# Linear attention feeding a two-matrix layer on one core: attention's products regrouped by array form, projection rounds of 4, 2 and 3 tiles

## The chip, the cores and the metric

The kernel runs on one core of a Trainium2 chip. The metric is the device time of one execution in microseconds; lower is better. Before the change the median of three runs is 1205.09 us (1204.46 to 1205.18).

## The reference

What is computed, cut to what matters (8 batches, 8 heads, 576 positions, head width 64, 128 features; the layer has 512 inputs and 2048 hidden units):

```python
def phi(x):
    proj = np.einsum('bhsd,df->bhsf', x, w_phi)
    proj = proj - np.max(np.abs(proj), axis=-1, keepdims=True)
    return np.concatenate([np.exp(proj), np.exp(-proj)], axis=-1)
q_p, k_p = (phi(q), phi(k))
kv = np.einsum('bhsf,bhsd->bhfd', k_p, v)
z = np.sum(k_p, axis=2)
num = np.einsum('bhsf,bhfd->bhsd', q_p, kv)
den = np.einsum('bhsf,bhf->bhs', q_p, z)[..., None] + 1e-06
attn = num / den
# heads side by side give x, 4608 tokens x 512
h = x @ w_in
out = (h - np.tanh(h)) @ w_out
```

## The kernel before, in words

There are two stages. In the first, attention is worked through in 32 units; a unit is one pair of heads of one batch. In the second stage the two-matrix layer runs over twelve groups of three token tiles and sixteen slices of the hidden width; the change touches it in one place only (where the last unit's reciprocal is taken). The second stage's weights come as 64-bit numbers and are turned into 32-bit ones on the way through the first stage (`dec_load`, `dec_0`, `dec_1`, `dec_2`).

The first stage runs in periods, written out by hand in `period(i)` under `tc.manual_schedule()`: each engine, and SP's queue of transfers, gets its instructions in the order of the text. A period works on four units at once: `a` = unit i (projected), `c` = unit i - 1 (its features are transposed, its products with v are summed), `p` = unit i - 2 (its numerator and denominator are formed), `p2_` = unit i - 3 (its division is finished).

The steps of a unit, by function and line of the profile:

- `load` and `load_v` (L184, L188) bring q and k (tile `qk`) and `v` of the next unit on SP's queue. Both tiles have two buffers.
- `project(u, r)` (L197) multiplies three tiles of q or k with `w_phi` on PE, a product for each of the two heads on its half of the rows (form 64x128), into the one buffer `pp` of PSUM. VectorE then takes the greatest absolute value (L202) and subtracts it (L204). There are three rounds, r = 0, 1, 2; four and a half of the nine tiles are q's.
- `qt` (L210) and `qt_rest` (L216) transpose q's part on PE; `q_exp` and `q_exp_rest` (L221, L226) take the exponentials on ScalarE into `qe`. `k_exp` (L231) does it for k, into `kp`.
- `kv` (L239) and `ksum` (L247) form the products of k's features with v (forms 128x64, and 64x64 for the half tile) and their sums (128x32 and 64x32), both in `pc`. `kv_copy` (L253) and `kv_turn` (L258, L260) copy and transpose them.
- `out_heads` forms the numerators (L268, form 128x64) and the denominators (L279, form 128x32) in three buffers `po`; `out_copy` (L289, L292) copies them out.
- `den` (L297) loads the denominators from `dd`, spread over all 128 partitions, as `dn`. `den_recip` adds the small constant and takes the reciprocal on VectorE (L305, L306), stores it in memory as `rr` (L307) and loads it back, one row for each head, as `rb` (L310). `den_mul` multiplies on POOL (L315) and stores the result in `xs` (L316), from which the second stage loads its x (L105).

All these transfers go out on SP's queue. A transfer waits there for what it needs, a full buffer to send or a free buffer to fill. The order on it in one period before the change: `qk` and `v` of unit i + 1, `dn` of `p`, `xs` of `p2_`, a weight (`raw`), then `rr` and twice `rb` of `p`.

Single-precision products are two instructions each on PE, and transposes one: that is why a round of six products shows as 12.

Of the kernel before, what the change touches and what calls it, by code (L numbers as in the profile page):

```python
# [19 lines left out]
P = 128  # L20
# [12 lines left out]
def tile_linear_attention_moe(  # L33
# [83 lines left out]
    with ExitStack() as c1:  # L117
# [40 lines left out]
        def dec_0(u):  # L158
            rr = u.r.bitcast(U32).rearrange("p (n t) -> p n t", t=2)
            u.lo, u.hi = rr[:, :, 0], rr[:, :, 1]  # L160
            u.a = raw.tile([P, DM], U32, tag="dec_a", name=f"dec_a{u.nm}", bufs=2)
            nc.scalar.activation(f32(u.a), f32(u.hi), AF.Abs, scale=65536.0)

        def dec_1(u):
# [14 lines left out]

        def load(u):  # L180
            u.qk = p2.tile([P, PC], F32, tag="qk", name=f"qk{u.i}")
            w = PC if u.i else 3 * P
            for o in range(0, PC, w):
                nc.sync.dma_start(u.qk[:, o : o + w], qkT[u.i][:, o : o + w])  # L184

        def load_v(u):
            u.v = p2.tile([P, 5, 2, D], F32, tag="v", name=f"v{u.i}")
            nc.sync.dma_start(u.v.rearrange("p j e d -> p (j e d)"), v5[u.i])  # L188


        def project(u, r):
            pp = ps_pj.tile([P, 2, 512], F32, tag="pj", name=f"pp{u.i}_{r}")
            for a in range(3):
                j = 3 * r + a
                for e in range(2):
                    hs = slice(e * D, (e + 1) * D)
                    nc.tensor.matmul(  # L197
                        pp[:, e, a * F : (a + 1) * F], u.qk[hs, j * P : (j + 1) * P], wph[hs, :], start=True, stop=True
                    )
            x = pp[:, :, 0 : 3 * F].rearrange("p e (a f) -> p e a f", f=F)  # L200
            m = p2.tile([P, 2, 3], F32, tag="m", name=f"m{u.i}_{r}")
            nc.vector.tensor_reduce(m, x, AX.X, ALU.max, apply_absolute_value=True)  # L202
            t = p2.tile([P, 2, 3, F], F32, tag=f"t{r}", name=f"t{u.i}_{r}")
            nc.vector.tensor_tensor(t, x, m.unsqueeze(3).broadcast_to([P, 2, 3, F]), ALU.subtract)  # L204
            u.t[r] = t

        def qt(u, e):
            pt = ps_tr.tile([P, 512], F32, tag="tr", name=f"ptt{u.i}_{e}")
            for j in range(4):
                nc.tensor.transpose(pt[:, j * P : (j + 1) * P], u.t[j // 3][:, e, j % 3, :], ident)  # L210
            return pt

        def qt_rest(u):
            pt = ps_tr.tile([P, 512], F32, tag="tr", name=f"ptr{u.i}")
            for e in range(2):
                nc.tensor.transpose(pt[:, e * SR : (e + 1) * SR], u.t[1][0:SR, e, 1, :], ident[0:SR, 0:SR])  # L216
            return pt

        def q_exp(u, e, pt):
# [6 lines left out]
                nc.scalar.activation(u.qe[:, :, s, SM:S], x, AF.Exp, scale=1.0 - 2.0 * s)  # L226

        def k_exp(u, r):
            x, j0, j1 = (u.t[1][:, :, 1:3, :], 0, 2) if r == 1 else (u.t[2], 2, 5)
            for s in range(2):  # L230
                nc.scalar.activation(u.kp[:, :, j0:j1, s, :], x, AF.Exp, scale=1.0 - 2.0 * s)  # L231


        def kv(u):
            u.pc = ps_c.tile([P, 512], F32, tag="pc", name=f"pc{u.i}")
            for j in range(5):
                r = slice(SR, P) if j == 0 else slice(0, P)
                for e in range(2):
                    nc.tensor.matmul(  # L239
                        u.pc[e * D : (e + 1) * D, 0 : 2 * F], u.v[r, j, e, :], u.kp[r, e, j, :, :], start=(j == 0), stop=(j == 4)  # L240
                    )

        def ksum(u):
            for j in range(5):
                r = slice(SR, P) if j == 0 else slice(0, P)
                for n in range(4):
                    nc.tensor.matmul(  # L247
                        u.pc[n * 32 : (n + 1) * 32, 2 * F : 3 * F], ones[r, :], u.kp[r, n // 2, j, n % 2, :], start=(j == 0), stop=(j == 4)
                    )

        def kv_copy(u):
            u.kvt = p2.tile([P, 3, F], F32, tag="kvt", name=f"kvt{u.i}")
            u.kv_last = nc.scalar.copy(u.kvt.rearrange("p a f -> p (a f)"), u.pc[:, 0 : 3 * F])  # L253

        def kv_turn(u):
            pt = ps_d.tile([P, 512], F32, tag="po", name=f"ptk{u.i}")
            for a in range(3):
                nc.tensor.transpose(pt[:, a * P : (a + 1) * P], u.kvt[:, a, :], ident)  # L258
            u.kv = p2.tile([P, 3, P], F32, tag="kv", name=f"kv{u.i}")
            nc.vector.tensor_copy(u.kv.rearrange("p a c -> p (a c)"), pt[:, 0 : 3 * P])  # L260


        def out_heads(u):
            u.po = [ps_d.tile([P, 512], F32, tag="po", name=f"po{u.i}_{c}") for c in range(3)]
            for s in range(2):
                for c in range(2):
                    for e in range(2):
                        nc.tensor.matmul(  # L268
                            u.po[c][e * D : (e + 1) * D, 0:CH],
                            u.kv[:, s, e * D : (e + 1) * D],  # L270
                            u.qe[:, e, s, c * CH : (c + 1) * CH],
                            start=(s == 0),
                            stop=(s == 1),
                        )
            for s in range(2):
                for e in range(2):
                    for c in range(2):
                        n, w = 2 * e + c, 2 * e + s
                        nc.tensor.matmul(  # L279
                            u.po[2][n * 32 : (n + 1) * 32, 0:CH],  # L280
                            u.kv[:, 2, w * 32 : (w + 1) * 32],
                            u.qe[:, e, s, c * CH : (c + 1) * CH],
                            start=(s == 0),
                            stop=(s == 1),
                        )

        def out_copy(u):
            u.dd = tail.tile([P, CH], F32, tag="dd", name=f"dd{u.i}", bufs=2)
            nc.scalar.copy(u.dd, u.po[2][:, 0:CH])  # L289
            u.d = tail.tile([P, S], F32, tag="d", name=f"d{u.i}", bufs=2)  # L290
            for c in range(2):
                nc.scalar.copy(u.d[:, c * CH : (c + 1) * CH], u.po[c][:, 0:CH])  # L292

        def den(u):
            w = 2 * S // P
            dn = tail.tile([P, w], F32, tag="dn", name=f"dn{u.i}")
            nc.sync.dma_start(dn, u.dd.rearrange("(n r) c -> n r c", r=32)[:, 0, :])  # L297
            u.dn = dn
# [33 lines left out]
        def unit(i):  # L332
            return units[i] if 0 <= i < NU else None


        def period(i):
            a, c, p, p2_ = unit(i), unit(i - 1), unit(i - 2), unit(i - 3)
# [3 lines left out]
            if i == NU - 2:  # L341
                xt[0] = x_tiles(0)
                for j in range(NCT):
                    x_load(0, xt[0], j)
            if a:
                a.kp = p2.tile([P, 2, 5, 2, F], F32, tag="kp", name=f"kp{i}")
                if i == 0:
                    warm(16)
                project(a, 0)
            if c:  # L350
                k_exp(c, 2)
            if p:
                out_heads(p)
            if 2 <= i < NU:
                dec_0(dec[i])
                dec_1(dec[i])
            if p:
                out_copy(p)
                den(p)
            if p2_:  # L360
                den_mul(p2_)
            if 1 <= i <= 2 * AHEAD:
                split_w(i - 1)
            if i < 2:
                warm(8)
            if c and i == 1:
                kv(c)
            if a:
                project(a, 1)
            if c and i > 1:  # L370
                kv(c)
            if a:
                k_exp(a, 1)
            if 2 <= i < NU:
                dec_2(dec[i])
            if 2 <= i < NU - 2:
                dec.append(dec_load(i + 2))
            if i == 0:
                warm(8)
            if a:  # L380
# [1 line left out]
            if i < 2:  # L382
                dec_0(dec[i])
                dec_1(dec[i])
                dec_2(dec[i])
                dec.append(dec_load(i + 2))
            if c:
                c.qe = p1.tile([P, 2, 2, S], F32, tag="qe", name=f"qe{i - 1}")
                pt = qt(c, 0)
                q_exp(c, 0, pt)  # L390
                ksum(c)
                ptr = qt_rest(c)
                kv_copy(c)
                q_exp_rest(c, ptr)
                pt = qt(c, 1)
                kv_turn(c)
                q_exp(c, 1, pt)
            if p:
                den_recip(p)
            if i == NU - 1:  # L400
                for j in range(NCT):
                    x_split(xt[0], j)
# [2 lines left out]
        with tc.manual_schedule():  # L405
            for i in range(NU + 1):
                period(i)
        period(NU + 1)

    with ExitStack() as c2:
# [68 lines left out]
        for i in range(len(steps) + 2):  # L481
# [12 lines left out]
            if 1 <= i <= len(steps):  # L494
                g, f = steps[i - 1]
                gg[i - 1] = split_g(g, f, gs.pop(i - 1), G)
            if i == 2:
                den_mul(units[-1], pin)
            while late and late[0] <= 2 * AHEAD + i * NL // (NF - 1):
# [61 lines left out]
```

## Time and profile before

| | |
|---|---|
| median of the runs | 1205.09 us |
| the profiled execution | 1203.97 us |
| its span | 1202.0 us |
| PE busy | 1181.3 us, 98% |
| VectorE (DVE) busy | 881.3 us, 73% |
| ScalarE (ACT) busy | 804.7 us, 67% |
| POOL busy | 288.8 us, 24% |
| first product of the second stage | at 384.25 us |
| one period of the first stage | 11.39 us |

Times in the profile count from the start of the span. PE is TensorE's products, PEld its weight loads, which can run beside the products; SPq is SP's queue, POOL is GpSimd. A line such as `L239 PE MATMUL pc<-kp,v 128*64 128x256` names the line of the kernel, the engine, the operation, the tile written and those read, the form in the array (rows used x columns used) and the size of what streams through. In the timeline and in the chain of waits the first number is the start, the second the time until the end of the last of the instructions drawn together, and `x12` says how many they are. A note in brackets such as `[0.28 <-DVE t L204]` is the engine's idle time ahead of it and who ended it. A matmul's end is modelled, so that neighbours overlap a little; the chain of waits cuts the overlap off.

### The profile page before, as it was taken

What the parts mean: (1) busy time and instruction counts of PE and PEld (TensorE: products, weight loads), DVE (VectorE), ACT (ScalarE), POOL (GpSimd) and SP (SyncE); (2) the same over time, 40 slices, a digit from 0 to 9 for tenths busy, and PEclk for the clock granted to TensorE, in tenths of its full rate; (3) what the DMA queues carried; (4) which work ended last, traced back from release to release, by engine and by line L of the source; (5) the groups of instructions that cost most, each with busy time, mean ns of one, the idle gap of its engine ahead of it and who ended that gap; (6) DMA issues with size and microseconds to landing.
All of it is one profiled execution on the core that took longest, in us unless ns stands there. A gap on an engine that the chain in (4) does not pass through costs nothing.

```text
span 1202.0 us, 22462 instructions
## 1 busy us (share of the span) xinstructions
PE 1181.3 (98%) x8584; PEld 967.1 (80%) x8584; DVE 881.3 (73%) x1458; ACT 804.7 (67%) x1716; POOL 288.8 (24%) x266
## 2 busy tenths in 40 slices
PE   7999999999999999999999999999999999999998
PEld 5666666666666788999999999999999999999997
DVE  5778877777775997777776777777776777777665
ACT  3666675665666776766776667777666777667665
POOL 0122121011011663222222222222222222222222
PEclk8999999999999999999999999999999999999999
DMA  4566566566563100000000100000000101000000
GB/s 151 162 176 192 167 189 185 163 201 179 168 205 93 34 14 34 21 34 14 31 17 14 40 14 33 20 34 14 34 20 7 40 14 40 14 27 1 28 1 26
DMA packets 51179, 85.69 MB, mean 71 GB/s; under 512 B 13312, under 2 KB 28160, under 8 KB 51072
## 3 DMA queue, kind: packets, MB, share of 16 engines
q1 hardware_dynamic: 51072, 84.27, 22.9%
q8 instruction: 67, 1.10, 0.4%
q14 instruction: 40, 0.33, 0.1%
HBM read 65.08 MB, written 19.02 MB: 70 GB/s over the span
## 4 chain that ended last, share of the span: by engine, by line
PE 93%; DVE 3%; issue 1%; DMA 1%; POOL 0%; ACT 0%; DVEq 0%; SPq 0%; POOLq 0%; ACTq 0%
PE ph L428 32%; PE po L465 10%; PE po L463 10%; PE po L462 10%; PE pp L197 7%; PE pc L239 7%; PE po L268 5%; PE pc L247 4%; PE ptt L210 3%; PE po L279 3%; PE ptk L258 1%; DVE s L445 1%; PE ptr L216 1%; DVE s L449 1%; DMA dn<-dd 0%
## 5 line engine op out<-in xcount | busy, mean ns | idle before, releaser
L456 POOL TENSOR_TENSOR gl<-s,gh 128x384 fp32r<-128x384 f32 x192 | 197.9, 1031 | 568.9 <-ACT gh L455 563.0
L428 PE MATMUL ph<-xh,wli 128*128 128x384 f32 x768 | 259.3, 338 | 1.3 <-POOL wli L93 1.3
L428 PE MATMUL ph<-xh,whi 128*128 128x384 f32 x768 | 258.7, 337 | 0.0
L428 PE MATMUL ph<-xl,whi 128*128 128x384 f32 x768 | 257.9, 336 | 0.0
L435 ACT ACTIVATE y<-ph 128x384 f32<-128x384 f32 x192 | 94.4, 492 | 236.9 <-PE ph L428 236.9
L444 DVE SCALAR_TENSOR_TENSOR s<-s,y 128x384 f32<-128x384 f32 x192 | 108.0, 562 | 167.9 <-ACT s L437 167.9
L462 PE MATMUL po<-who,gh 128*128 128x512 f32 x576 | 227.3, 395 | 3.2 <-ACT gh L455 3.1
L463 PE MATMUL po<-wlo,gh 128*128 128x512 f32 x576 | 226.8, 394 | 0.0
L465 PE MATMUL po<-who,gl 128*128 128x512 f32 x576 | 164.3, 393 | 1.6 <-POOL gl L456 1.5
L449 DVE COPY_PREDICATED s<-mk,th 128x384 f32<-128x384 uint32 x192 | 140.3, 731 | 20.5 <-ACT y L435 0.5
L428 PEld LDWEIGHTS ph<-xh,whi 128*128 128x128 f32 x768 | 144.3, 188 | 8.9 <-issue 0.5
L428 PEld LDWEIGHTS ph<-xl,whi 128*128 128x128 f32 x768 | 144.2, 188 | 8.2
L428 PEld LDWEIGHTS ph<-xh,wli 128*128 128x128 f32 x768 | 144.0, 188 | 2.0 <-POOL wli L93 1.9
L231 ACT ACTIVATE kp<-t 128x768 f32<-128x768 f32 (+1 forms) x128 | 87.2, 733 | 67.3 <-DVE t L204 67.3
L465 PEld LDWEIGHTS po<-who,gl 128*128 128x128 f32 x576 | 107.8, 188 | 28.1 <-POOL gl L456 3.3
L445 DVE SCALAR_TENSOR_TENSOR s<-s,s 128x384 f32<-128x384 f32 x192 | 115.2, 600 | 19.3 <-ACT mk L443 0.5
L462 PEld LDWEIGHTS po<-who,gh 128*128 128x128 f32 x576 | 107.9, 187 | 22.6 <-ACT gh L455 5.6
L202 DVE TENSOR_REDUCE m<-pp 128x6 f32<-128x768 f32 x96 | 91.8, 956 | 45.3 <-PE pp L197 45.2
L443 ACT ACTIVATE mk<-y,bias_t 128x384 f32<-128x384 f32 x192 | 117.9, 614 | 6.5 <-DVE s L449 6.3
L463 PEld LDWEIGHTS po<-wlo,gh 128*128 128x128 f32 x576 | 108.2, 188 | 16.3
L439 ACT ACTIVATE s<-y,bias_t 128x384 f32<-128x384 f32 x192 | 117.6, 612 | 1.4 <-POOL gl L456 1.3
L437 ACT ACTIVATE s<-y,bias_t 128x384 f32<-128x384 f32 x192 | 118.4, 617 | 0.0
(63 smaller groups left out, 1587.2 us busy)
## 6 DMA issues: line engine op xcount, KB each, us to landing
qk<-in_qkT SPq DMA_DIRECT2D x31, 576.0 KB, 4.8
v<-in_v SPq DMA_DIRECT2D x32, 320.0 KB, 4.1
rb<-rr SPq DMA_DIRECT2D x64, 144.0 KB, 3.3
xs<-rb SPq DMA_DIRECT2D x32, 288.0 KB, 4.1
x<-xs SPq DMA_DIRECT2D x48, 192.0 KB, 2.4
out<-o SPq DMA_DIRECT2D x36, 256.0 KB, 2.1
rawi<-in_moe_w_in SPq DMA_DIRECT2D x16, 512.0 KB, 4.2
rawo<-in_moe_w_out SPq DMA_DIRECT2D x16, 512.0 KB, 4.5
```

What stands on the lines that cost most here:

```text
L428: nc.tensor.matmul(h, wt[:, c * P : (c + 1) * P], x[:, c, 0:N], start=(i == 0), stop=(i == 3 * NCT - 1))
L435: nc.scalar.activation(y, h, AF.Square)
L437: nc.scalar.activation(s1, y, AF.Square, bias=bias_t[:, 0:1])
L439: nc.scalar.activation(s2, y, AF.Square, bias=bias_t[:, 1:2])
L443: nc.scalar.activation(mk, y, AF.Relu, bias=bias_t[:, 2:3])
L444: nc.vector.scalar_tensor_tensor(s1, s1, PC1, y, ALU.add, ALU.mult)
L445: nc.vector.scalar_tensor_tensor(s2, s2, PC2, s1, ALU.add, ALU.mult)
L449: nc.vector.copy_predicated(gs, mk.bitcast(U32), th)
L456: pin(nc.gpsimd.tensor_tensor(gl, gs, f32(gh), ALU.subtract))
L462: nc.tensor.matmul(po[t], a, wo[f][0], start=(f == 0), stop=False)
L463: nc.tensor.matmul(po[t], a, wo[f][1], start=False, stop=False)
L465: nc.tensor.matmul(po[t], gl[:, t * P : (t + 1) * P], wo[f][0], start=False, stop=(f == NF - 1))
```

## The change

The order of the products in a period is another one, and some functions are split so that it can be.

On PE the order before was: round 0, numerators, denominators, round 1, `kv`, round 2, `qt(0)`, `ksum`, `qt_rest`, `qt(1)`, `kv_turn`. It becomes: round 0 (four tiles), `num` of `p`, `kv` of `c`, round 1 (two tiles), `qt_rest`, `qt(0)`, `qt(1)`, `turn`, round 2 (three tiles), `denom` of `p`, `ksum` of `c`. The half tile of `kv` and `ksum` comes last of its five instead of first. Since `ksum(c)` is now at the end of its period, its sums are copied at the start of the next (`ksum_copy`) and transposed together with the next unit's products (`turn`), and the denominators of `p` follow in the same period (`denom`).

Since the denominators are finished at the end of the period, their way through memory begins in the next: `den_recip_load(p2_)` stands behind round 0 and `k_exp(c, 2)`, `den_recip(p2_)` and `den_mul(p2_)` behind `kv(c)` and ahead of round 1. The order on SP's queue in one period becomes: `qk` and `v` of unit i + 1, `dn`, `rr`, twice `rb` and `xs`, all four of `p2_`, then `raw`.

Buffers: `dec_a` and the third round's `t` go from two to one, `kvt` and `kv` as well, `qe` from one to two; `qt_rest` writes into the buffers `po` instead of `tr`. The first unit's load is cut at four and six tiles instead of every three.

The diff, cut to its core:

```diff
-            w = PC if u.i else 3 * P
-            for o in range(0, PC, w):
-                nc.sync.dma_start(u.qk[:, o : o + w], qkT[u.i][:, o : o + w])
+            cut = (0, PC) if u.i else (0, 4 * P, 6 * P, PC)
+            for o, w in zip(cut, cut[1:]):
+                nc.sync.dma_start(u.qk[:, o:w], qkT[u.i][:, o:w])
...
+        ROUNDS = ((0, 4), (4, 6), (6, 9))
+
         def project(u, r):
+            j0, j1 = ROUNDS[r]
+            n = j1 - j0
...
         def qt_rest(u):
-            pt = ps_tr.tile([P, 512], F32, tag="tr", name=f"ptr{u.i}")
+            pt = ps_d.tile([P, 512], F32, tag="po", name=f"ptr{u.i}")
...
+        KT = (1, 2, 3, 4, 0)
+
         def kv(u):
             u.pc = ps_c.tile([P, 512], F32, tag="pc", name=f"pc{u.i}")
-            for j in range(5):
+            for j in KT:
...
         def kv_copy(u):
-            u.kvt = p2.tile([P, 3, F], F32, tag="kvt", name=f"kvt{u.i}")
-            u.kv_last = nc.scalar.copy(u.kvt.rearrange("p a f -> p (a f)"), u.pc[:, 0 : 3 * F])
+            u.kvt = p1.tile([P, 2, F], F32, tag="kvt", name=f"kvt{u.i}")
+            nc.scalar.copy(u.kvt.rearrange("p a f -> p (a f)"), u.pc[:, 0 : 2 * F])
+
+        def ksum_copy(u):
+            if u.i < NU - 1:
+                u.kst = p1.tile([P, F], F32, tag="kst", name=f"kst{u.i}")
+            else:
+                u.kst = p2.tile([P, PC], F32, tag="qk", name=f"kst{u.i}")[:, 0:F]
+            nc.scalar.copy(u.kst, u.pc[:, 2 * F : 3 * F])
+
+        def turn(c, ks):
+            i = c.i if c else ks[0].i + 1
+            pt = ps_d.tile([P, 512], F32, tag="po", name=f"ptk{i}")
+            src = [c.kvt[:, s, :] for s in range(2)] if c else []
+            src += [u.kst for u in ks]
+            for a, x in enumerate(src):
+                nc.tensor.transpose(pt[:, a * P : (a + 1) * P], x, ident)
+            t = p1.tile([P, 4, P], F32, tag="kv", name=f"kv{i}")
+            n = len(src)
+            nc.vector.tensor_copy(t[:, 0:n, :].rearrange("p a c -> p (a c)"), pt[:, 0 : n * P])
...
-        def out_heads(u):
-            u.po = [ps_d.tile([P, 512], F32, tag="po", name=f"po{u.i}_{c}") for c in range(3)]
+        def num(u):
+            u.po = [ps_d.tile([P, 512], F32, tag="po", name=f"po{u.i}_{c}") for c in range(2)]
...
+        def denom(u):
+            u.pd = ps_d.tile([P, 512], F32, tag="po", name=f"pd{u.i}")
...
-        def den(u):
+        def den_recip_load(u):
             w = 2 * S // P
             dn = tail.tile([P, w], F32, tag="dn", name=f"dn{u.i}")
             nc.sync.dma_start(dn, u.dd.rearrange("(n r) c -> n r c", r=32)[:, 0, :])
...
+        def q_side(c):
+            c.qe = p2.tile([P, 2, 2, S], F32, tag="qe", name=f"qe{c.i}")
+            pts = [qt_rest(c), qt(c, 0), qt(c, 1)]
+            q_exp_rest(c, pts[0])
+            for e in range(2):
+                q_exp(c, e, pts[1 + e])
...
         def period(i):
             a, c, p, p2_ = unit(i), unit(i - 1), unit(i - 2), unit(i - 3)
...
+            if p:
+                ksum_copy(p)
...
                 project(a, 0)
             if c:
                 k_exp(c, 2)
-            if p:
-                out_heads(p)
+            if p2_:
+                den_recip_load(p2_)
             if 2 <= i < NU:
                 dec_0(dec[i])
                 dec_1(dec[i])
             if p:
-                out_copy(p)
-                den(p)
+                num(p)
+                num_copy(p)
+            if c:
+                kv(c)
+                if i == NU:
+                    ksum(c)
+                    ksum_copy(c)
             if p2_:
+                den_recip(p2_)
                 den_mul(p2_)
             if 1 <= i <= 2 * AHEAD:
                 split_w(i - 1)
             if i < 2:
                 warm(8)
-            if c and i == 1:
-                kv(c)
             if a:
                 project(a, 1)
-            if c and i > 1:
-                kv(c)
+            if c:
+                kv_copy(c)
+                q_side(c)
+                turn(c, ([p] if p else []) + ([c] if i == NU else []))
             if a:
                 k_exp(a, 1)
...
             if a:
                 project(a, 2)
...
+            if p:
+                denom(p)
+                denom_copy(p)
+            if c and i < NU:
                 ksum(c)
...
-        period(NU + 1)
+        for u in units[-2:]:
+            den_recip_load(u)
+        den_recip(units[-2])
+        den_mul(units[-2])
...
+            if i == 1:
+                den_recip(units[-1], pin)
             if i == 2:
                 den_mul(units[-1], pin)
```

More of the change, by code (lines that the diff above doesn't have):

```diff
@@ L160, in dec_0 @@
             u.lo, u.hi = rr[:, :, 0], rr[:, :, 1]
-            u.a = raw.tile([P, DM], U32, tag="dec_a", name=f"dec_a{u.nm}", bufs=2)
+            u.a = raw.tile([P, DM], U32, tag="dec_a", name=f"dec_a{u.nm}", bufs=1)
             nc.scalar.activation(f32(u.a), f32(u.hi), AF.Abs, scale=65536.0)
@@ L188, in load_v @@
             nc.sync.dma_start(u.v.rearrange("p j e d -> p (j e d)"), v5[u.i])
+        ROUNDS = ((0, 4), (4, 6), (6, 9))
         def project(u, r):
+            j0, j1 = ROUNDS[r]
+            n = j1 - j0
             pp = ps_pj.tile([P, 2, 512], F32, tag="pj", name=f"pp{u.i}_{r}")
-            for a in range(3):
-                j = 3 * r + a
+            for a in range(n):
+                j = j0 + a
                 for e in range(2):
@@ L199, in project @@
                     )
-            x = pp[:, :, 0 : 3 * F].rearrange("p e (a f) -> p e a f", f=F)
-            m = p2.tile([P, 2, 3], F32, tag="m", name=f"m{u.i}_{r}")
+            x = pp[:, :, 0 : n * F].rearrange("p e (a f) -> p e a f", f=F)
+            m = p2.tile([P, 2, n], F32, tag=f"m{r}", name=f"m{u.i}_{r}")
             nc.vector.tensor_reduce(m, x, AX.X, ALU.max, apply_absolute_value=True)
-            t = p2.tile([P, 2, 3, F], F32, tag=f"t{r}", name=f"t{u.i}_{r}")
-            nc.vector.tensor_tensor(t, x, m.unsqueeze(3).broadcast_to([P, 2, 3, F]), ALU.subtract)
+            t = p2.tile([P, 2, n, F], F32, tag=f"t{r}", name=f"t{u.i}_{r}", bufs=1 if r == 2 else 2)
+            nc.vector.tensor_tensor(t, x, m.unsqueeze(3).broadcast_to([P, 2, n, F]), ALU.subtract)
             u.t[r] = t
@@ L209, in qt @@
             for j in range(4):
-                nc.tensor.transpose(pt[:, j * P : (j + 1) * P], u.t[j // 3][:, e, j % 3, :], ident)
+                nc.tensor.transpose(pt[:, j * P : (j + 1) * P], u.t[0][:, e, j, :], ident)
             return pt
         def qt_rest(u):
-            pt = ps_tr.tile([P, 512], F32, tag="tr", name=f"ptr{u.i}")
+            pt = ps_d.tile([P, 512], F32, tag="po", name=f"ptr{u.i}")
             for e in range(2):
-                nc.tensor.transpose(pt[:, e * SR : (e + 1) * SR], u.t[1][0:SR, e, 1, :], ident[0:SR, 0:SR])
+                nc.tensor.transpose(pt[:, e * SR : (e + 1) * SR], u.t[1][0:SR, e, 0, :], ident[0:SR, 0:SR])
             return pt
@@ L228, in k_exp @@
         def k_exp(u, r):
-            x, j0, j1 = (u.t[1][:, :, 1:3, :], 0, 2) if r == 1 else (u.t[2], 2, 5)
+            x, j0, j1 = (u.t[1], 0, 2) if r == 1 else (u.t[2], 2, 5)
             for s in range(2):
                 nc.scalar.activation(u.kp[:, :, j0:j1, s, :], x, AF.Exp, scale=1.0 - 2.0 * s)
+        KT = (1, 2, 3, 4, 0)
         def kv(u):
             u.pc = ps_c.tile([P, 512], F32, tag="pc", name=f"pc{u.i}")
-            for j in range(5):
+            for j in KT:
                 r = slice(SR, P) if j == 0 else slice(0, P)
@@ L239, in kv @@
                     nc.tensor.matmul(
-                        u.pc[e * D : (e + 1) * D, 0 : 2 * F], u.v[r, j, e, :], u.kp[r, e, j, :, :], start=(j == 0), stop=(j == 4)
+                        u.pc[e * D : (e + 1) * D, 0 : 2 * F], u.v[r, j, e, :], u.kp[r, e, j, :, :], start=(j == KT[0]), stop=(j == KT[-1])
                     )
         def ksum(u):
-            for j in range(5):
+            for j in KT:
                 r = slice(SR, P) if j == 0 else slice(0, P)
@@ L247, in ksum @@
                     nc.tensor.matmul(
-                        u.pc[n * 32 : (n + 1) * 32, 2 * F : 3 * F], ones[r, :], u.kp[r, n // 2, j, n % 2, :], start=(j == 0), stop=(j == 4)
+                        u.pc[n * 32 : (n + 1) * 32, 2 * F : 3 * F], ones[r, :], u.kp[r, n // 2, j, n % 2, :], start=(j == KT[0]), stop=(j == KT[-1])
                     )
         def kv_copy(u):
-            u.kvt = p2.tile([P, 3, F], F32, tag="kvt", name=f"kvt{u.i}")
-            u.kv_last = nc.scalar.copy(u.kvt.rearrange("p a f -> p (a f)"), u.pc[:, 0 : 3 * F])
[L255 to L260, printed above, removed]
-        def out_heads(u):
-            u.po = [ps_d.tile([P, 512], F32, tag="po", name=f"po{u.i}_{c}") for c in range(3)]
+            u.kvt = p1.tile([P, 2, F], F32, tag="kvt", name=f"kvt{u.i}")
[17 more added lines that the diff above has]
+            if c:
+                c.kv = t
+            for a, u in enumerate(ks):
+                u.ks = t[:, n - len(ks) + a, :]
+        def num(u):
+            u.po = [ps_d.tile([P, 512], F32, tag="po", name=f"po{u.i}_{c}") for c in range(2)]
             for s in range(2):
@@ L279, in out_heads @@
                         nc.tensor.matmul(
-                            u.po[2][n * 32 : (n + 1) * 32, 0:CH],
-                            u.kv[:, 2, w * 32 : (w + 1) * 32],
+                            u.pd[n * 32 : (n + 1) * 32, 0:CH],
+                            u.ks[:, w * 32 : (w + 1) * 32],
                             u.qe[:, e, s, c * CH : (c + 1) * CH],
@@ L285, in out_heads, with num_copy @@
                         )
-        def out_copy(u):
-            u.dd = tail.tile([P, CH], F32, tag="dd", name=f"dd{u.i}", bufs=2)
-            nc.scalar.copy(u.dd, u.po[2][:, 0:CH])
+        def num_copy(u):
             u.d = tail.tile([P, S], F32, tag="d", name=f"d{u.i}", bufs=2)
@@ L292, in out_copy, with denom_copy @@
                 nc.scalar.copy(u.d[:, c * CH : (c + 1) * CH], u.po[c][:, 0:CH])
-        def den(u):
+        def denom_copy(u):
+            u.dd = tail.tile([P, CH], F32, tag="dd", name=f"dd{u.i}", bufs=2)
+            nc.scalar.copy(u.dd, u.pd[:, 0:CH])
+        def den_recip_load(u):
             w = 2 * S // P
@@ L365, in period @@
                 warm(8)
-            if c and i == 1:
-                kv(c)
             if a:
                 project(a, 1)
-            if c and i > 1:
-                kv(c)
+            if c:
+                kv_copy(c)
+                q_side(c)
+                turn(c, ([p] if p else []) + ([c] if i == NU else []))
             if a:
                 k_exp(a, 1)
[L374 to L377, printed above, removed]
             if i == 0:
@@ L384, in period @@
                 dec_1(dec[i])
+            if i < NU:
                 dec_2(dec[i])
+            if i < NU - 2:
                 dec.append(dec_load(i + 2))
[L387 to L390, printed above, removed]
+            if p:
+                denom(p)
+                denom_copy(p)
+            if c and i < NU:
                 ksum(c)
[L392 to L399, printed above, removed]
+            if i == NU:
+                num(c)
+                num_copy(c)
+                denom(c)
+                denom_copy(c)
             if i == NU - 1:
```

## The prediction

> **What bounds the kernel now.** I read a table by stretches of time first, then the chain of waits over one period of the attention stage, then the queue of SP, and last the places where a wait on `dn` shows.
>
> ```profile
> 200.00:250.00 50.00, 50.00 (x618) 31.79 (x616) 38.93 (x60) 31.85 (x67) 5.64 (x4) 1.00 0.57 173
> ```
>
> The row is 50 us in the middle of the attention stage: PE is busy for all 50, VectorE 38.93, ScalarE 31.85, at a granted clock of 1.00. So in this stage only PE's own work, or a new wait of PE, can move the time. The chain of waits over one period (start, duration, what):
>
> ```profile
> 211.07 0.87 PE pp L197 x12
> 211.94 2.09 PE po L268 x16
> 214.03 1.11 PE po L279 x16
> 215.14 0.87 PE pp L197 x12
> 216.01 2.46 PE pc L239 x20
> 218.46 0.87 PE pp L197 x12
> 219.33 0.59 PE ptt L210 x4
> 219.92 1.36 PE pc L247 x40
> 221.28 0.26 PE ptr L216 x2
> 221.54 0.59 PE ptt L210 x4
> 222.13 0.33 PE ptk L258 x3
> 222.46 0.87 PE pp L197 x12
> ```
>
> It is PE from end to end; a period is 222.46 - 211.07 = 11.39 us, with no wait in it. What a change of array form costs is seen in the timeline of PE, looked at in narrow windows so that single products show (start, duration):
>
> ```profile
> 211.21 0.50 PE L197 MATMUL pp<-wph,qk 64*128 64x128 f32 x6
> 211.67 0.27 PE L197 MATMUL pp<-wph,qk 64*128 64x128 f32 x1
> 216.79 0.59 PE L239 MATMUL pc<-kp,v 128*64 128x256 f32 x3
> 218.08 0.38 PE L239 MATMUL pc<-kp,v 128*64 128x256 f32 x1
> 218.39 0.38 PE L197 MATMUL pp<-wph,qk 64*128 64x128 f32 x2
> ```
>
> A projection round of three tiles is six pairs of products. Between 211.21 and 211.67 lie four pitches, 0.112 us each; the whole round is 0.87, so six pitches (0.67) leave 0.20 for getting in and out. For `kv` six pitches lie between 216.79 and 218.08, 0.215 each, and its last step, to 218.39, is 0.31: 0.10 to get out. So leaving a form costs about 0.10 and entering one up to 0.10; for the entries that go away I take half, 0.05.
>
> **The change, part by part: PE's own work.** I rebuild the period from the chain's durations, taking 0.10 off where a stretch is no longer left and 0.05 where it is no longer entered. Round 0 with four tiles: 0.87 + 2 x 0.112 = 1.09. `num`, followed by the same form: 2.09 - 0.10 = 1.99. `kv`, entered from the same form, its half-height part now last: 2.46 - 0.05 = 2.41. Round 1 with two tiles, followed by `qt_rest` in the same form: 0.87 - 0.22 - 0.10 = 0.55. `qt_rest` 0.26. Both `qt` and `turn` together: 0.59 + 0.59 + 0.33 - 0.15 = 1.36. Round 2: 0.87. `denom`: 1.11 - 0.10 = 1.01. `ksum`: 1.36 - 0.05 = 1.31. Sum 10.85, so 0.54 us a period less, if PE waits for nothing. Were `qt_rest` after a round a change of form all the same, 0.1 to 0.2 of that would go.
>
> **The step that is moved: the denominator's way through memory.** Before, `den(p)` issues the load of `dn` in one period, and VectorE reads it last in that period. After it, `den_recip_load(p2_)` stands early in the period, but behind `load_v` on the same queue; and `den_recip(p2_)` stands on VectorE ahead of round 1's reduce and subtract. What SP's queue does in the trace (the waits of SP: who waited for whom, us in total, times, longest; then the timeline):
>
> ```profile
> SPq L188 <- PE pc L239: 48.8, 21, 3.2
> ```
>
> ```profile
> 218.50 0.33 SPq L188 DMA_DIRECT2D v<-in_v  x1
> 218.93 0.59 SPq L297 DMA_DIRECT2D dn<-dd  x1
> ```
>
> In 21 of 21 periods the load of `v` (L188) waited for `kv` (L239): `v` has two buffers, so v(i+1) takes the one that `kv(c)` of this very period reads. It goes out 0.11 us after the next round begins (218.39 to 218.50), and `dn` stands behind it: 0.43 later, although its source had been copied long before. Today this is free, since VectorE takes `dn` up last in the period, behind the copy of `kv`'s turned products (which need `ptk`, 222.13 in the chain above), some 4 us after the issue. The change leaves `load_v` first in the period and takes that cover away.
>
> After the change, from the start of round 0: `kv` ends and round 1 starts at 1.09 + 1.99 + 2.41 = 5.49; `v` goes out at 5.60, `dn` at 6.03, and lands D later. Only then can VectorE take the reciprocal, then round 1's reduce and subtract, then the one projection buffer is free for round 2, which PE reaches at 5.49 + 0.55 + 0.26 + 1.36 = 7.66. The trace of before has this chain once, near the stage's end, where four loads of x push `dn` late (timeline, then the chain of waits):
>
> ```profile
> 355.14 0.33 SPq L188 DMA_DIRECT2D v<-in_v  x1
> 355.53 1.85 SPq L105 DMA_DIRECT2D x<-xs  x4
> 361.08 0.17 DVE L305 TENSOR_SCALAR rn<-dn 128x9 f32<-128x9 f32 x1 [1.38 <-DMA dn<-dd]
> 361.53 0.32 SPq L307 DMA_DIRECT2D rr<-rn  x1
> ```
>
> ```profile
> 357.48 3.50 DMA dn<-dd
> 361.50 0.82 DVE m L202
> 363.45 0.94 PE pp L197 x12
> 384.81 1.97 DMA dn<-dd
> ```
>
> VectorE sat 1.38 us for `dn`, and PE's next round came late. From landing (357.48 + 3.50 = 360.98) to the reduce is 0.52, from there through the subtract to PE's next round 1.95 (363.45). Round 1 now has 512 elements a partition where reduce and subtract took this long for 768:
>
> ```profile
> L204 DVE TENSOR_TENSOR t<-pp,m 128x768 f32<-128x768 f32 x61 | 58.4, 957 | 2.1
> ```
>
> A third of 957 ns off each of the two is 0.64 us (0 if nothing were saved by the smaller size), so 1.95 becomes 1.31. Round 2 can start at 6.03 + D + 0.52 + 1.31 = 7.86 + D, against 7.66: PE waits 0.20 + D, and the period is **A = 10.85 + 0.20 + D = 11.05 + D**. Against 11.39 the change gains only if D is under 0.34 us. The two rows above give D: 1.97 with nothing ahead of it, 3.50 behind large loads. A is 13.0 to 14.6.
>
> **A second loop: SP's queue.** `dn`, `rr`, `rb`, `xs`, then `raw`, `qk`, `v` and the next `dn` now stand in one row on SP, and each of the first four waits for the one before. Before, `xs` of an older unit stood between and overlapped. Sizes (page) and times (timeline at the stage's end):
>
> ```profile
> qk<-in_qkT SPq DMA_DIRECT2D x31, 576.0 KB, 4.8
> v<-in_v SPq DMA_DIRECT2D x32, 320.0 KB, 4.1
> xs<-rb SPq DMA_DIRECT2D x32, 288.0 KB, 4.1
> x<-xs SPq DMA_DIRECT2D x48, 192.0 KB, 2.4
> rawi<-in_moe_w_in SPq DMA_DIRECT2D x16, 512.0 KB, 4.2
> ```
>
> ```profile
> 381.35 0.32 SPq L307 DMA_DIRECT2D rr<-rn  x1
> 382.77 1.11 SPq L310 DMA_DIRECT2D rb<-rr  x2
> 388.04 0.32 SPq L316 DMA_DIRECT2D xs<-rb  x1
> ```
> From `dn`'s landing to `rr` 0.55 (360.98 to 361.53), from `rr` to `xs` 388.04 - 381.35 = 6.69. Then xs + raw + qk + v, 288 + 512 + 576 + 320 = 1696 KB, lie ahead of the next `dn`. The nearest rate: 320 + 4 x 192 = 1088 KB went out from 355.14 and the `dn` behind landed at 360.98, 5.84 us; less 1.42 for a small transfer by itself (`rr` to the `rb` that waits for it, 381.35 to 382.77) that is 4.42 us, so 1696 KB take 6.89. **B = 0.55 + 6.69 + 1.42 + 6.89 = 15.55 us.** Its other end is a queue that has drained by the time `v` goes out; then it bounds nothing and A with D = 1.97 does.
>
> I take 15.2: between A's upper end (14.6, D behind large loads, which is the row nearest to this case) and B, and nearer B, since a slower PE clock (below) can only lift A.
>
> **Edits at nothing.** `ksum_copy` is one ScalarE copy more, and ScalarE has 18 of 50 us free. `dec_a` with one buffer: `dec_0` comes on ScalarE behind `k_exp(c, 2)`, two activations that start with the same subtract after which VectorE runs `dec_2`, so it isn't late. `turn`'s copy comes behind round 1's subtract, and `denom` needs it only after round 2. The first load cut otherwise, and the tail of the stage, whose waits for `dn` and for the turned products stay, I take as 0, give or take the 1.97 us of `dn`'s last landing. The second stage is untouched.
>
> **Sum.** `dn` is waited for with a round behind it in periods 3 to 31: 29 x (15.2 - 11.39) = +110. Periods 1 and 2 gain 0.54 each: -1. Against the profiled execution, 1203.97: 1313. The median is 1.1 above that execution, so 1314.
>
> **A clock that falls.** At the start of the kernel PE once waited for the same subtract:
>
> ```profile
> 23.37 0.94 PE L197 MATMUL pp<-wph,qk 64*128 64x128 f32 x12 [2.14 <-DVE t L204]
> ```
>
> ```profile
> 24.00:28.00 4.00, 4.00 (x53) 2.57 (x50) 3.52 (x6) 2.42 (x5) 0.00 (x0) 0.57 0.00 0
> ```
>
> After a pause of 2.14 us the next 4 us ran at a granted clock of 0.57. A pause of 0.20 + D (2.2 to 3.7) in each period may do so each time: up to 0.43 x 4 = 1.7 us, which loop B partly hides; A with it is up to 16.3. The Trainium skill (TensorE: Matmul & The Clock Gate, Part 1) says the opposite of so short a pause: the clock falls after at least one idle window of about 3.4 us. By that rule A stays at 14.6 or under and the time at 1204 + 29 x 3.2 = 1297 where B doesn't bind; the row here bears the rule out poorly, since 2.14 us were enough.
>
> **The rivals.** (1) *The queue is drained when `v` goes out, and the clock holds*: D = 1.97, A = 13.0; 29 x 1.6 - 1 = +46, so 1251. For it: SP then waits for `kv` some us with raw and qk on their way. Against: in `dn`'s other row, large loads made it 3.50. (2) *Faster: `dn` has landed when VectorE comes to it.* PE runs without a wait, 31 x 0.54 = 17, so 1188. It decides if `dn` goes out ahead of `v`'s wait, some 2 us before VectorE has done round 0. Against it are the 21 of 21 waits and SP's rows, which stand in the order of the text. (3) *The clock falls in every period and the queue is slower*: a period of 16.3 to 17, so 29 x 4.9 - 1 = +141 to 29 x 5.6 - 1 = +161, 1346 to 1366. (4) *No cheaper forms*: the stall swallows it; A is up to 0.5 longer, B as it is; the time is that of the forecast.
>
> **How the numbers follow.** Forecast, period 14 to 16.3 (1280 to 1346), with (4) in it: 0.70. Rival 1: 0.14. Rival 3: 0.08. Rival 2: 0.06; within 0.2%, about what a measurement can tell here: 0.02. The range runs from rival 1 less a little, 1248, to rival 3, 1365; what lies out is rival 2, no change, and tails. Slower 0.92, same 0.02, faster 0.06.
>
> **What would show it.** Right: idle time of PE ahead of round 2 of 2 us or more a period, put down to VectorE's subtract; VectorE waiting for `dn` ahead of L305; `v` still released by `kv`; fewer and shorter gaps at changes of form (10.85 us of PE work a period); granted clock under 1.00 in the attention stage if rival 3 is at work. Wrong: `dn` issued ahead of `v`, VectorE never idle on it, PE dense at a period of 10.9.

## The result, and the profile after

| | before | after |
|---|---|---|
| median of six runs each | 1204.62 us | 1309.95 us (1305.43 to 1316.88) |
| the profiled execution, its span | 1203.97, 1202.0 us | 1310.60, 1308.8 us |
| first product of the second stage | 384.2 us | 489.9 us |
| granted clock over the span | 0.997 | 0.966 |

The ratio is 1.0878, interval 1.0844 to 1.0913: slower. Of the 106.8 us that the span grew, 105.7 lie before the second stage begins, so the loss is attention's alone. The predicted 1314 was 4 us off.

The chain of waits after the change, one period from round 2 to round 2 (start, duration, what):

```profile
213.61 1.65 PE pp L202 x12
215.26 1.81 PE pd L306 x16
217.06 1.23 PE pc L254 x40
218.29 1.09 PE pp L202 x16
219.38 2.09 PE po L291 x16
221.47 2.33 PE pc L246 x20
...
223.88 0.36 ACT kvt L260
224.24 2.75 DMA dn<-dd
...
227.02 0.18 DVE rn L334
...
227.44 0.56 DVE m L207
...
228.02 0.70 DVE t L209
...
228.86 0.94 PE pp L202 x12
```

Where the chain of before was PE from end to end, here it leaves PE behind `kv` and comes back 5 us later, over the load of `dn`, the reciprocal, round 1's reduce and its subtract. The period is 228.86 - 213.61 = 15.25 us; before it was 11.39.

The chain names ScalarE's copy of `kvt` as what came before the load. That is only what ended last beforehand. The timeline of the same place shows what held the load on SP's queue:

```profile
223.71 0.71 PE L202 MATMUL pp<-wph,qk 64*128 64x128 f32 x8
223.82 0.33 SPq L188 DMA_DIRECT2D v<-in_v  x1
224.24 0.59 SPq L326 DMA_DIRECT2D dn<-dd  x1
227.02 0.17 DVE L334 TENSOR_SCALAR rn<-dn 128x9 f32<-128x9 f32 x1 [3.58 <-DMA dn<-dd]
228.86 0.94 PE L202 MATMUL pp<-wph,qk 64*128 64x128 f32 x12 [2.97 <-DVE t L209]
```

`v` goes out 0.11 us after round 1 begins, that is when `kv` has freed its buffer, and `dn` 0.42 behind it. VectorE idles 3.58 us for `dn`, PE then 2.97 us for the subtract. Over 300 us the waits add up to this (who waited for whom: us, times, longest; the second is from SP's own list):

```profile
DVE rn L334 <- DMA dn<-dd: 73.5, 20, 4.7
PE pp L202 <- DVE t L209: 61.3, 20, 4.1
```

```profile
SPq L188 <- PE pc L246: 55.7, 20, 4.6
```

These are twenty periods: PE waits 3.07 us in each, and SP itself waits 2.8 for `kv`. From the reciprocal at 91.80 us to the one twenty periods later, at 394.95, the mean period is 15.2 us. The table by stretches shows the third part, the clock (0.87 in the column behind POOL's, where it was 1.00 before):

```profile
200.00:250.00 50.00, 41.15 (x487) 27.96 (x479) 27.07 (x41) 24.53 (x53) 7.26 (x6) 0.87 0.40 128
```

The clock doesn't fall behind every pause. From 100 to 150 us it is granted in full, and two rounds there start behind pauses that are hardly shorter (table by stretches, then timeline):

```profile
100.00:150.00 50.00, 38.72 (x479) 26.46 (x474) 30.40 (x48) 29.35 (x63) 9.03 (x7) 1.00 0.48 159
```

```profile
122.69 0.94 PE L202 MATMUL pp<-wph,qk 64*128 64x128 f32 x12 [2.88 <-DVE t L209]
136.24 0.94 PE L202 MATMUL pp<-wph,qk 64*128 64x128 f32 x12 [2.68 <-DVE t L209]
```

From one round to the other are 13.55 us: 2.68 of waiting and 10.87 of PE's own work. Between 60 and 460 us, round 2, `denom` and `ksum` together take 3.20 us behind 7 of the 26 pauses (these are 2.62 to 2.88 us long) and 4.6 to 6.0 behind the other 19 (2.66 to 4.10 long). So the mean period adds up: 10.87 of work, 3.07 of waiting and some 1.2 for products at the lower clock are about 15.2. Against the 11.39 of before, the change wins 0.5 of work and loses 4.3.

### The profile page after: what moved, and what is told of

It reads as the page before. It is cut to its first block, busy times and chain, and to the rows that moved or that the text cites. A ratio compares the mean times of both kernels' runs of the same rounds, so it can differ in the third digit from the quotient of the medians.

```text
span 1308.8 us, 22549 instructions
## 1 busy us (share of the span) xinstructions
PE 1202.1 (92%) x8584; PEld 993.6 (76%) x8584; DVE 873.8 (67%) x1458; ACT 815.0 (62%) x1748; POOL 289.4 (22%) x266
## 4 chain that ended last, share of the span: by engine, by line
PE 83%; DMA 7%; DVE 6%; ACT 2%; issue 1%; POOL 1%; SPq 0%; DVEq 0%; ACTq 0%; POOLq 0%
PE ph L471 29%; PE po L508 10%; PE po L506 10%; PE po L505 10%; DMA dn<-dd 6%; PE pp L202 6%; PE pc L246 6%; PE po L291 5%; PE pd L306 4%; PE pc L254 4%; DVE t L209 2%; DVE m L207 2%; ACT kvt L260 1%; DVE rn L335 0%; DVE s L488 0%
## 5 line engine op out<-in xcount | busy, mean ns | idle before, releaser
L202 PE MATMUL pp<-wph,qk 64*128 64x128 f32 x1152 | 99.7, 309 | 92.8 <-DVE t L209 89.4
L202 PEld LDWEIGHTS pp<-wph,qk 64*128 64x128 f32 x1152 | 80.9, 205 | 119.9 <-issue 117.0
L207 DVE TENSOR_REDUCE m<-pp 128x8 f32<-128x1024 f32 (+2 forms) x96 | 90.2, 940 | 94.5 <-PE pp L202 94.5
L344 POOL TENSOR_TENSOR rb<-d,rb 128x576 f32<-128x576 f32 x32 | 47.6, 1489 | 407.9 <-DMA rb<-rr 298.4
L488 DVE SCALAR_TENSOR_TENSOR s<-s,s 128x384 f32<-128x384 f32 x192 | 115.2, 600 | 19.7 <-ACT mk L486 0.9
```

The lines of the kernel that those rows point to most:

```text
L202: nc.tensor.matmul(pp[:, e, a * F : (a + 1) * F], u.qk[hs, j * P : (j + 1) * P], wph[hs, :], start=True, stop=True)
L488: nc.vector.scalar_tensor_tensor(s2, s2, PC2, s1, ALU.add, ALU.mult)
```

## The experiments

Two theories went in. W: VectorE waits for `dn`, which stands behind `v`, which waits for `kv`. Q: the denominator's four transfers and the loads, in one row on SP's queue, are a loop of their own. Rivals: the regrouping itself, its buffers or its rounds are what costs (R), and the fallen clock (C).

**The moved step alone, in the old order of products** (label moved_alone).

```diff
 # the kernel before
             if c:
                 k_exp(c, 2)
+            if p2_:
+                den(p2_)
             if p:
                 out_heads(p)
...
                 out_copy(p)
-                den(p)
             if p2_:
+                den_recip(p2_)
                 den_mul(p2_)
...
-            if p:
-                den_recip(p)
```

> The old order of PE's products and the old rounds of three tiles; only the denominator's way is moved as in the change: dn is loaded behind round 0 of the next period, and the reciprocal stands on VectorE ahead of round 1's reduce. Theory W (VectorE waits for dn, which stands on SP's queue behind v, and v waits for kv): here kv ends later, v goes out about 7.4 us into the period, dn at 7.9; with D = 2.8 it lands at 10.7, round 1's reduce starts at 11.2 and round 2 at 13.2 where PE could have had it at 7.4. A wait of 5.8 us, a period of 17.2, 1204 + 29 x 5.8 = 1372, and up to 2 us a period more for a fallen clock: 1372 to 1430. Rival R (the new order of products or the unequal rounds are what costs): nothing of that is in this kernel, so 1205.

Measured 1434.02 against 1203.22 us, ratio 1.1902 (1.1871 to 1.1933). Timeline:

```profile
203.89 0.33 SPq L188 DMA_DIRECT2D v<-in_v  x1
204.31 0.59 SPq L297 DMA_DIRECT2D dn<-dd  x1
206.75 0.17 DVE L305 TENSOR_SCALAR rn<-dn 128x9 f32<-128x9 f32 x1 [6.20 <-DMA dn<-dd]
209.12 1.66 PE L197 MATMUL pp<-wph,qk 64*128 64x128 f32 x12 [5.28 <-DVE t L204]
```

None of the regrouping is in this kernel, and it loses twice as much: the moved step is enough for the loss, and R isn't needed. (That the regrouping itself loses nothing is shown only by the kernel with the queue in order, below.) The wait was foretold as 5.8 and is 5.3; the period is 19.7 us, 8.3 longer than before, so that the clock took some 3 us where 2 were allowed for it (a round of 0.87 us takes 1.66 behind the pause), and the time lies 4 us over the range. The new order of products, in which `kv` ends 2 us earlier in the period, made the moved step cheaper, not dearer.

**A third buffer for `v`** (label v3).

```diff
-            u.v = p2.tile([P, 5, 2, D], F32, tag="v", name=f"v{u.i}")
+            u.v = p2.tile([P, 5, 2, D], F32, tag="v", name=f"v{u.i}", bufs=3)
...
-            u.dd = tail.tile([P, CH], F32, tag="dd", name=f"dd{u.i}", bufs=2)
+            u.dd = tail.tile([P, CH], F32, tag="dd", name=f"dd{u.i}", bufs=1)
...
-            rb = tail.tile([P, S], F32, tag="rb", name=f"rb{u.i}", bufs=2)
+            rb = tail.tile([P, S], F32, tag="rb", name=f"rb{u.i}", bufs=1)
```

> The changed kernel with three buffers for v in place of two, so that v need not wait for this period's kv (dd and rb have one buffer each to make room; both are long free when they are written again). Theory W alone: dn goes out early, VectorE doesn't wait, a period of 10.85, 1188. Theory Q (SP's queue, in which dn, rr, rb, xs and then raw, qk, v and the next dn wait in a row, is a second bound, loop B of the prediction): 7.4 us from dn's landing to xs, then 1696 KB ahead of the next dn: a period of 14.0 (334 GB/s) to 15.7 (251 GB/s), 1280 to 1330, with SP never waiting for kv.

Measured 1291.57 us, ratio 1.0717 (1.069 to 1.0745), 14.6 us a period (19 periods from 100.12 to 378.42 us). The wait behind `v` is gone (`kv` is not in SP's list of waits any more), and yet only 18 of 105 us came back. Timeline:

```profile
200.85 0.17 DVE L334 TENSOR_SCALAR rn<-dn 128x9 f32<-128x9 f32 x1 [1.40 <-DMA dn<-dd]
201.31 0.32 SPq L336 DMA_DIRECT2D rr<-rn  x1
202.72 1.11 SPq L339 DMA_DIRECT2D rb<-rr  x2
207.73 1.42 POOL L344 TENSOR_TENSOR rb<-d,rb 128x576 f32<-128x576 f32 x1 [12.29 <-DMA rb<-rr]
209.17 0.33 SPq L345 DMA_DIRECT2D xs<-rb  x1
...
211.17 0.59 SPq L326 DMA_DIRECT2D dn<-dd  x1
216.67 0.17 DVE L334 TENSOR_SCALAR rn<-dn 128x9 f32<-128x9 f32 x1 [4.81 <-DMA dn<-dd]
```

This is loop Q by itself, in one of its longer periods: from one `dn` in hand to the next `dn` asked for, 10 us of waits in a row; and that `dn` then lands 5.5 us later, behind `xs`, a weight, `qk` and `v`, all issued in the 2 us ahead of it (over twenty periods VectorE takes it up 3.6 to 6.7 us after its issue, 4.9 on average). W alone is refuted as the whole cause.

**`dn` ahead of the loads** (label dn_first).

```diff
+            if p2_:
+                den_recip_load(p2_)
             if i + 1 < NU:
                 load(units[i + 1])
...
                 k_exp(c, 2)
-            if p2_:
-                den_recip_load(p2_)
```

> The changed kernel with dn's load ahead of qk and v at the top of the period; one step moved, and v still waits for kv. Theory W alone: dn lands before VectorE comes to it, 1188. With theory Q beside it: rr now stands behind v's wait (5.6 us into the period), then rr, rb, POOL and xs take it to 14.5, raw to 14.9, and the next dn lands behind xs and raw some 4.6 later: a wait of PE of about 1.4 us, a period of 12.3, 1230.

Measured 1258.05 us, ratio 1.0439 (1.0406 to 1.0472), 13.3 us a period: slower than both theories together said (1230), faster than the change. Two reciprocals in a row (timeline), and `v`'s wait (SP's list, 280 us):

```profile
203.18 0.17 DVE L334 TENSOR_SCALAR rn<-dn 128x9 f32<-128x9 f32 x1 [2.15 <-DMA dn<-dd]
216.51 0.17 DVE L334 TENSOR_SCALAR rn<-dn 128x9 f32<-128x9 f32 x1 [2.86 <-DMA dn<-dd]
```

```profile
SPq L188 <- PE pc L246: 10.2, 8, 2.7
```

From reciprocal to reciprocal 13.33 us, and VectorE waits for `dn` at both. `v` waits for `kv` in 8 periods only, half a microsecond a period: SP comes to it too late for that. I had worked out 12.3 with `v`'s wait inside the loop; the loop closed without it and was 1 us longer. Moving one step within the row doesn't open it.

**Filling the pause** (label fill).

```diff
+            if a and p2_:
+                for _ in range(40):
+                    nc.tensor.matmul(c.pc[:, 3 * F : 4 * F], zt[:, 0:P], zt[:, 0:P], start=True, stop=True)
             if a:
                 project(a, 2)
```

> The changed kernel with 40 small products of zeros (128 columns, 16-bit) into an unused part of pc just ahead of round 2, in periods 3 to 31, to keep PE at work in the pause. They take some 2.2 us of a pause of 3. Theory C (of a period of 15.0 us about 11.05 + 2.8 = 13.85 is the wait behind v, and the other 1.2 us is PE at about half speed after the pause): the granted clock stays near 1.00 and the period falls to 13.9, 1310 - 29 x 1.15 = 1277. Theory Q (SP's queue binds at about 15): clock near 1.00, but the time stays at 1310, the pause only growing longer.

Measured 1302.59 us, ratio 1.0814 (1.0777 to 1.0851): 7 us better than the change, where their intervals just touch, of 33 that theory C promised. The clock rose only to 0.985 over the span, since a pause stays:

```profile
207.09 2.40 PE L423 MATMUL pc<-zt 128*128 128x128 bf16 x40
209.63 0.17 DVE L334 TENSOR_SCALAR rn<-dn 128x9 f32<-128x9 f32 x1 [3.98 <-DMA dn<-dd]
211.47 0.94 PE L202 MATMUL pp<-wph,qk 64*128 64x128 f32 x12 [1.99 <-DVE t L209]
212.34 2.15 PE L306 MATMUL pd<-qe,kv 128*32 128x288 f32 x16
```

`denom` still takes 2.15 in this period (1.18 at full clock). Over 19 periods VectorE waits 78.5 us for `dn`, 4.1 each where it was 3.7: what PE won was in part given back to the queue, where `dn` is now taken up 3.4 us after its issue and not 2.9. This run doesn't settle how much the clock alone costs; the sum of the period in the section on the result does, with some 1.2 us.

**The queue in another order** (label queue_order). All engines keep the change's order; on SP `dn` comes first, then the store of the unit before, `qk`, `rr` and `rb`, then `v`, then the weight.

```diff
         def den_mul(u, pin=lambda ins: ins):
             x = u.rb
             pin(nc.gpsimd.tensor_tensor(x, u.d, x, ALU.mult))
+
+        def store_x(u):
+            x = u.rb
             nc.sync.dma_start(xs[u.b // 2][u.hp, :, (u.b % 2) * S : (u.b % 2 + 1) * S], x)
...
+            if p2_:
+                den_recip_load(p2_)
+            if p3_:                      # p3_ = unit(i - 4)
+                store_x(p3_)
             if i + 1 < NU:
                 load(units[i + 1])
-                load_v(units[i + 1])
...
-            if p2_:
-                den_recip_load(p2_)
...
             if p2_:
                 den_recip(p2_)
+            if i + 1 < NU:
+                load_v(units[i + 1])
+            if p2_:
                 den_mul(p2_)
```

> The changed kernel with SP's queue put in an order in which nothing waits for long: dn at the top of the period, then the store of the unit before (xs, one period later than its product on POOL), qk, rr and rb, then v, then raw. PE, ScalarE and VectorE keep the changed order. Theory W + Q (the loss is the wait behind v and the row of waits on SP's queue, nothing else): PE runs dense again, a period of 10.85, 1205 - 31 x 0.54 = 1188. Rival (the fuller ScalarE order or the tighter buffers, dec_a and kv with one each, hold PE up as well): a period of 11.4 or more, 1205 or slower.

Measured 1193.37 against 1205.03 us, ratio 0.9906 (0.9892 to 0.9921): faster than both kernels, by 117 us than the change. Its chain of waits over one period:

```profile
201.94 0.94 PE pp L202 x12
202.88 1.11 PE pd L306 x16
203.98 1.23 PE pc L254 x40
205.21 1.09 PE pp L202 x16
206.30 2.09 PE po L291 x16
208.39 2.31 PE pc L246 x20
210.70 0.65 PE pp L202 x8
211.34 0.11 PE ptr L221 x2
211.45 1.03 PE ptt L215 x8
212.48 0.34 PE ptk L276 x3
212.82 0.13 issue
212.95 0.94 PE pp L202 x12
```

PE from end to end again, 11.01 us a period, and no wait of VectorE for `dn`. The loss was the queue's order and what follows from it, the waits and the lower clock; with that mended, fewer changes of form are worth 0.38 us a period. The expected 1188 was missed by 5: the pause of 0.13 to 0.2 us ahead of round 2 (round 1's reduce and subtract are just too long for the transposes that cover them) is 0.17 x 31 = 5.

**`v` left where it was** (label store_later). As the one before, but `load_v` stays behind `load` at the top of the period.

> As the kernel with the queue put in order, but v stays at the top of the period behind qk, so that rr and rb still wait behind v and so behind this period's kv; only dn goes first and xs one period later. If a chain of waits on SP's queue only costs when it is longer than the period: rr goes out at 6.0, rb at 8.9, POOL is done at 14.4, that is 3.6 into the next period, and xs, qk and v still go out in time: 1188 to 1195. If v's wait itself is what costs wherever it stands ahead of the denominator's steps: 1230 or slower, as with dn's load first alone (1258).

Measured 1201.39 us, ratio 0.9962 (0.9948 to 0.9976). The time lies between the two expectations. `v` still waits for `kv` ahead of the denominator's steps (14 times in 26 periods, 14.1 us in all), and this kernel is still a little faster than before. So `v`'s wait by itself doesn't cost what it cost in the change; that it costs where the row behind it is longer than the period is the reading that fits. Here the row is just about that long: ScalarE's copy of the numerators waited 46.9 us in those 26 periods for POOL to free `d`, more than the near tie I had worked out.

**One join undone** (label rest_apart), from the kernel with the queue in order; on ScalarE the exponentials of `qt_rest` move behind those of `qt` with it:

```diff
-            pts = [qt_rest(c), qt(c, 0), qt(c, 1)]
+            pts = [qt(c, 0), qt(c, 1), qt_rest(c)]
```

> As the kernel with the queue put in order, with qt_rest behind qt(0) and qt(1) instead of ahead of them, so that it stands apart from round 1: two changes of array form more in a period and nothing else. By the prices of the prediction (0.10 out, 0.05 to 0.10 in) each costs 0.15 to 0.20, so 0.3 to 0.4 a period: 31 x 0.35 = 11 us slower than the kernel with the queue in order. If a change of form costs nothing by itself, no difference.

Measured 1195.35 us, ratio 0.9925 (0.9914 to 0.9937), 2.0 us slower than with the join. Timeline:

```profile
209.97 0.71 PE L202 MATMUL pp<-wph,qk 64*128 64x128 f32 x8
210.62 1.09 PE L215 MATMUL ptt<-ident,t 128*128 128x128 f32 x8
211.64 0.34 PE L221 MATMUL ptr<-ident,t 64*128 64x64 f32 x2
...
212.39 0.94 PE L202 MATMUL pp<-wph,qk 64*128 64x128 f32 x12
```

Round 1 to round 2 takes 2.42 us without a pause. With the join it took 212.95 - 210.63 = 2.32, of which about 0.2 is the pause: 2.1 of work. So two changes of form cost 0.3, as priced; but 0.2 of it fills a pause that stands there anyway, and so 2 us of the expected 11 show. The price was right, and that it would show in the time was wrong.

## Why the prediction was right, point by point

- *PE's own work, 10.85 us a period.* Shown twice: 10.87 in the changed kernel where the clock held, and 11.01 with a pause of 0.13 to 0.2 in the kernel with the queue in order. The prices of a change of form, about 0.15 in and out, held in the last experiment.
- *The moved step.* Shown: `v` released by `kv` in 20 of 20 periods, `dn` 0.42 us behind it, VectorE and then PE idle for it. The formula A = 11.05 + D stands: PE's wait of 3.07 is 0.20 + D with D = 2.9 (2.89 and 2.75 us in the two periods looked at). Even the 0.20 is there by itself as the pause that is left when D is hidden.
- *D was mis-sized.* I took the row with 1088 KB ahead, 3.50. It is 2.9, since SP waits 2.8 us for `kv` and the queue drains meanwhile. The other kernels bear that out: `dn` is taken up 2.5 us after its issue where SP waits 7.8 us for `kv` (the moved step alone), and 4.9 after it where `v` doesn't wait (the third buffer). A is 13.9, not 14.6. The other row, 1.97, was misread: there is something ahead of it, two loads of `rb` of 144 KB each, issued from 382.77 us on.
- *The clock was mis-sized the other way.* I left it out of the sum and let it only lift A. PE's work fills 15.16 - 3.07 = 12.1 us a period where it is 10.87 at full clock: 1.2 us. A and the clock together make the 15.2 that was measured; 15.2 was predicted from A's upper end and B. So rival 3 was half right, in the clock (behind 19 of 26 pauses) and not in the queue.
- *Loop B was over-sized.* 15.55 was worked out; in the kernel with three buffers it is 14.6. It isn't what bound the change, where `v` waits for `kv` in every period, but it stands half a microsecond behind, and so taking away the wait behind `v` alone gained so little. The place and the mechanism were right. That the number came so close is luck: a D too long and a B too long stood in for a clock that wasn't counted.
- *One period too many.* The sum counts periods 3 to 31. Period 31 has no `v` to load, and in the trace VectorE doesn't wait for `dn` there (the reciprocal at 471.08 us): 28 periods, not 29, which is about the 4 us by which the forecast was too long.
- *Edits at nothing* (`ksum_copy`, one `dec_a`, the tighter buffers, the cut of the first load, the tail): shown for the first three, which are in the kernel that runs at 11.01 us a period. The first load and the tail come to nothing together: in that kernel the second stage begins at 372.3 us in place of 384.2, 11.9 earlier, and 31 periods of 0.38 less are 11.8 of it.
- *The clock rule.* The pauses here are 2.97 and 3.11 us, and the products behind them run at about half speed for a while (`pd` 1.81 in the chain, 1.11 in the kernel with the queue in order). The Trainium skill (TensorE: Matmul & The Clock Gate, Part 1) asks for an idle window of about 3.4 us for that; here, as at the start of the kernel before, shorter pauses were enough. They weren't always: a pause of 2.66 us was followed by slow products and one of 2.88 wasn't, so that the length of the pause alone doesn't tell.

## What to carry to other kernels

When a step is moved, walk its transfers along the queue that issues them: each one waits behind every earlier one, and a load that waits for a buffer of this very period holds up all that follows. Then close the loop: a row of transfers that wait for one another is a period of its own, and mending one link of it helps only until the next link binds. Where PE's order is improved, put the queue's order right first; the same regrouping was worth +8.8% with the one order and -0.9% with the other.

## What the runs showed that was not expected

A pause of PE costs twice: in the kernel with the moved step alone the waits are 5.3 us a period, and the period grew by 8.3. And how long a transfer of 4.5 KB takes depends on what its queue has just sent: `dn` was taken up 2.5 us after its issue where SP had stood still for 7.8 us ahead of `v`, 2.9 where it had stood for 2.8, and 4.9 where `xs`, a weight, `qk` and `v` went out right ahead of it.
